# Global queries' scores of a batch in one stage of eight array parts, with masks by two engines, later taps and the second half of the tokens first

## The chip, the cores and the metric

The kernel runs on one core of one Trainium2 chip. The metric is device time in microseconds of one execution; lower is better. Five engines work beside each other and each runs its own instructions in order: TensorE (PE in the profile, PEld for its weight loads), VectorE (DVE), ScalarE (ACT), GpSimd (POOL) and SyncE (SP), which here only issues the DMA transfers.

## What is computed

Attention with 32 global and 512 local tokens per head, then a gated feed-forward block with a convolution of three taps over the tokens. There are 8 batches, 8 heads, 64 numbers per head, 512 model columns and 1024 hidden columns. The reference, cut to what matters:

```python
k_all, v_all = concat([k_g, k_l]), concat([v_g, v_l])        # 32 + 512 tokens
out_g = softmax(scale * q_g @ k_all.T) @ v_all               # global queries see every token
s_ll  = where(abs(i - j) <= 32, scale * q_l @ k_l.T, -1e9)   # local queries: a window
out_l = softmax(concat([scale * q_l @ k_g.T, s_ll])) @ v_all
x = concat([out_g, out_l])                                   # tokens first, heads side by side: 544 rows of 512
h = maximum(x @ w_in, 0.0)
gate = 1 / (1 + exp(-conv3(h, conv_w)))
out = (h * gate) @ w_out
```

## The kernel before, in words

**Attention.** Two heads make a pair, with the first head's 64 numbers in partitions 0 to 63 and the second's in 64 to 127. One transfer (LQ, line 229) brings a pair's queries and its keys, another (LV, line 236) its values, and LG (line 242) four heads' global queries, padded with zeros so that one matmul over 128 partitions picks one head of a pair. The stages of a pair are S (scores, line 264, eight parts of the array of 64 rows x 32 columns), M (scale, mask and minimum on DVE, line 285, four blocks a head), E (exponential on ACT, line 295), T (transposes, line 304), A (copy out of PSUM), P (values, line 325, four parts of 128 x 32), N (division by the sums, line 333), U (transposes, line 341) and, for each half of the 544 tokens, XH and XL (the rounded value and the rest, line 364). Tokens 0 to 271 are the first half; the 32 global tokens are its head.

**Global queries.** For every four heads there is a chain of its own: G (scores against all keys, line 278: four matmuls of 480 columns and four of 64 in four parts of 128 x 32, into two PSUM banks), GM (scale and minimum, lines 373 to 377), GE (exponential), GN (one over the sums, into the small tile `gw`, lines 389 to 392), GT (six transposes, line 406), GC (copies into `pgt`), GP (values, line 422), GO (multiplies by `gw` and places the heads, line 429), GQ (line 436) and GX (lines 443 and 444), which writes the global tokens' columns of the first half. There are 16 such chains, two in a batch.

**Feed-forward.** A unit is 128 hidden columns of one half of a batch's tokens: PZ (twelve matmuls, line 460), RE (line 469), C1 (middle tap on POOL, line 248), Ca and Cb (outer taps on DVE, line 484), and for two units at a time TH (line 493), GG (line 498), GH and GL (the rounded product and the rest). Eight units make a half; then four output tiles follow, each of Oa and Ob (twelve matmuls each, line 523), OE (copy) and ST (store, line 536). The first half's units need GX, the second half's don't.

**Weights.** The weights come as 64-bit numbers in eight pieces of 1024 KB, four of w_in and four of w_out. WD loads a piece (line 174), WA takes its magnitude on ACT (line 112), WC (lines 119 to 123) and WL (lines 126 to 134) turn it on DVE into a rounded part and a rest, WH casts the rounded part on ACT. The taps are treated in the same way ahead of everything else (lines 149 to 159). A piece of w_in serves two units of each half, a piece of w_out one output tile.

**Masks.** POOL builds `corner` and copies it in 30 blocks into `mask` (lines 85 to 105), behind `place` and `whose`.

**Order.** A planner in the kernel (`plan`, `arranged`, `emit`) goes through all stages with a cost table and, for every kind of stage, a due time (`POS` for the batches from the second on, `POS0` for the first, `WPOS` for the weight pieces); the engine takes the most urgent stage that is ready and whose buffers are free (`SLOTS`: 8 PSUM banks, 3 qk, 3 vf, one pg, one pgt and so on). The order that comes out is then fixed on each engine.

Of the kernel before, what the change touches and what calls it, by code (L numbers as in the profile page):

```python
# [47 lines left out]
def f(ap):  # L48
    return ap.bitcast(F32)
# [3 lines left out]
def attn_moe(ctx: ExitStack, tc: tile.TileContext, qk_d, vw_d, qg_d, w_in_d, w_out_d, cw_d, out_d):  # L53
# [19 lines left out]

    place = const.tile([P, 2, SG], F32, name="place")
# [7 lines left out]

    corner = const.tile([P, 2, 4, SG], F32, name="corner")
    nc.gpsimd.memset(corner, 0.0)
    for k, sign in enumerate((1, -1)):
        nc.gpsimd.affine_select(
            out=corner[:, k], in_=corner[:, k], pattern=[[sign * SG, 4], [sign, SG]], compare_op=ALU.is_ge, fill=NEG,
            base=0, channel_multiplier=-sign,  # L90
        )
    mask = const.tile([P, 4, 4, SG], F32, name="mask")
    nc.gpsimd.memset(mask, 0.0)
    for i in range(NB):
        t, b = divmod(i, 4)
        rows = slice(b * SG, (b + 1) * SG)
        for k in range(4):
            block = FIRST[i] + k
            local = block - block // 4
            if block % 4 == 3 or local == i:  # L100
                continue
            if abs(local - i) > 1:
                nc.gpsimd.memset(mask[rows, t, k], NEG)
            else:
                nc.gpsimd.tensor_copy(out=mask[rows, t, k], in_=corner[rows, int(local > i), b])
# [22 lines left out]
    def rest(on, out, w0, w1, p, low):  # L128

        nc.vector.tensor_scalar(out=w1, in0=w1, scalar1=low, scalar2=None, op0=ALU.bitwise_and)  # L130
        v = nc.vector
        v.scalar_tensor_tensor(out=f(w1), in0=w0, scalar=2.0**-32, in1=w1, op0=ALU.mult, op1=ALU.add)  # L132
        if on == "v":
            v.scalar_tensor_tensor(out=out, in0=f(w1), scalar=2.0**-20, in1=f(p), op0=ALU.mult, op1=ALU.mult)
        else:
            nc.scalar.mul(out=f(p), in_=f(p), mul=2.0**-20)
            nc.gpsimd.tensor_tensor(out=out, in0=f(w1), in1=f(p), op=ALU.mult)
# [11 lines left out]
    nc.sync.dma_start(out=cwr.rearrange("p n w -> p (n w)"), in_=cw_d)  # L149
    cw = drop(cwr)  # L150
    if wpe == 2:
        cw = const.tile([P, 3 * NFT], F32, name="cw")
        cwp = const.tile([P, 3 * NFT], U32, name="cwp")
        w0, w1, t = cwr[:, :, 0], cwr[:, :, 1], cw.bitcast(U32)
        magnitude(w1, t)
        scaled_bits(w1, t, 0x7FFFF8)
        power(cwp, t)
        rest("v", f(cwp), w0, w1, cwp, 0)
        nc.vector.tensor_tensor(out=cw, in0=cw, in1=f(cwp), op=ALU.add)
# [24 lines left out]
    def WA(i):  # L184
        if wpe == 2:
            wf[i] = load.tile([P, 1024], U32, name="wt", bufs=SLOTS["wt"])
            magnitude(raw[i][:, :, 1], wf[i])

    def WC(i):
        if wpe == 2:  # L190
            scaled_bits(raw[i][:, :, 1], wf[i], 0x7FF000)
# [4 lines left out]
    def WL(i):  # L196
# [22 lines left out]
    groups = {}  # L219
    xs = {}  # L220
# [17 lines left out]
    def LG(n):  # L238
        b, h = divmod(n, H)
        gr = groups[n // 4] = {}  # L240
        gr["qgf"] = load.tile([P, 4, SG], F32, name="qgf", bufs=SLOTS["qg"])
        nc.sync.dma_start(out=gr["qgf"], in_=qg_d[b, h // 4])
# [26 lines left out]
    def G(n):  # L269

        gr = groups[n // 4]
        gr["s0"] = bank([P, 480], "psg0")
        gr["s1"] = bank([P, 64], "psg1")
        for i, ps in enumerate((gr["s0"], gr["s1"])):
            for j in range(4):
                k = heads[n - 3 + j // 2 * 2]["qk"][:, SL:]
                k = k[:, 608:672] if i else k[:, 0:640].rearrange("p (a c) -> p a c", c=P)[:, :, 0:96]
                nc.tensor.matmul(ps[j * SG : (j + 1) * SG], lhsT=gr["qgf"][:, j, :], rhs=k, start=True, stop=True)  # L278
# [107 lines left out]
    def GN(n):  # L386
# [4 lines left out]
        gr["w"] = small.tile([P, 2], F32, name="gw", bufs=SLOTS["pg"])  # L391
        nc.vector.tensor_scalar(out=gr["w"], in0=whose, scalar1=sums, scalar2=None, op0=ALU.mult)
# [22 lines left out]
    def GP(n):  # L415
        gr, first = groups[n // 4], n - 3
        po = gr["po"] = bank([P, D], "go")
        for c in range(6):
            for j in range(4):
                own = slice(j * SG, (j + 1) * SG)  # L420
                v = heads[first + j // 2 * 2]["vf"][:, j % 2, VALUES.index(ONCE[c]), :]
                nc.tensor.matmul(po[own], lhsT=gr["pgt"][:, c, own], rhs=v, start=c == 0, stop=c == 5)  # L422

    def GO(n):

        gr = groups[n // 4]
        og = gr["og"] = att.tile([P, 2, D], F32, name="og", bufs=SLOTS["pg"])
        po, w = gr["po"], gr["w"]
        nc.vector.tensor_tensor(
            out=og, in0=po[:, None, :].to_broadcast([P, 2, D]), in1=w[:, :, None].to_broadcast([P, 2, D]), op=ALU.mult  # L430
# [19 lines left out]

    def Z(u):
        hh, ft = divmod(u, NFT)
        b, half = divmod(hh, 2)
# [41 lines left out]
    def GG(u):  # L495
        t, half = hid[u]["two"], u // NFT % 2
# [30 lines left out]
    def OE(o):  # L527
        hh, mt = divmod(o, NCT)
        b, half = divmod(hh, 2)
# [3 lines left out]
    def ST(o):  # L533
        hh, mt = divmod(o, NCT)
        b, half = divmod(hh, 2)
# [7 lines left out]
        Oa=lambda o: O(o, 0), Ob=lambda o: O(o, 1), OE=OE, ST=ST, WD=WD, WA=WA, WC=WC, WH=WH, WL=WL,  # L543
# [5 lines left out]
    ps=8, x=13, hb=2, qk=3, vf=3, qg=2, p=4, r=3, a=4, n=2, pg=1, pgt=1, t=2, o=2, wt=1, g0=2, g1=2,  # L549
# [5 lines left out]
    A="a", GC="a", XH="a", GX="v", RE="a", C1="p", GH="a", GL="v", OE="v", WA="a", WH="a", WL="v",  # L555
)
ENG0 = dict(
    A="a", GC="a", XH="a", GX="v", RE="a", C1="p", GH="a", GL="p", OE="v", WA="a", WH="a", WL="v",
# [15 lines left out]
LATE = (17.01, 35.33)
# [346 lines left out]
```

## Time and profile before

| | |
|---|---|
| median of 3 runs | 595.16 us (594.88 to 595.27) |
| the profiled execution's own time | 595.32 us |
| its span, first to last instruction | 593.5 us |
| mean granted TensorE clock | 0.982 |
| PE busy | 560.9 us, 95% |
| DVE, ACT, POOL busy | 424.0, 324.2, 101.1 us |
| moved by DMA | 68.46 MB |

A row of a group names line, engine, operation, tiles written and read, sizes and count, then the busy time in us, the mean of one in ns, and the engine's idle time just ahead of it with what ended it. A row of the timeline gives start and length in us; several alike are merged, and a bracket at the end is idle time before it and its releaser. Matmuls are counted twice where they are of plain fp32: 128 matmuls of G are 256 records. Instructions of one engine overlap a little, so the distance from one start to the next is the measure of what one costs.

### The profile page before, as it was taken

What the parts mean: (1) busy time and instruction counts of PE and PEld (TensorE: products, weight loads), DVE (VectorE), ACT (ScalarE), POOL (GpSimd) and SP (SyncE); (2) the same over time, 40 slices, a digit from 0 to 9 for tenths busy, and PEclk for the clock granted to TensorE, in tenths of its full rate; (3) what the DMA queues carried; (4) which work ended last, traced back from release to release, by engine and by line L of the source; (5) the groups of instructions that cost most, each with busy time, mean ns of one, the idle gap of its engine ahead of it and who ended that gap; (6) DMA issues with size and microseconds to landing.
All of it is one profiled execution on the core that took longest, in us unless ns stands there. A gap on an engine that the chain in (4) does not pass through costs nothing.

```text
span 593.5 us, 20757 instructions
## 1 busy us (share of the span) xinstructions
PE 560.9 (95%) x8704; PEld 528.8 (89%) x8704; DVE 424.0 (71%) x1388; ACT 324.2 (55%) x994; POOL 101.1 (17%) x190
## 2 busy tenths in 40 slices
PE   5656997999999999999999999999999999999997
PEld 3345896999999999999999999999999999999997
DVE  4999999689477948577685858668584856565651
ACT  4954794676477666446565655555565543333320
POOL 6000242033012111121111012111101212221210
PEclk9977999899999999999999999999999999999999
DMA  6987334156234332123333222232412000000001
GB/s 254 390 286 313 95 118 170 39 204 223 91 135 153 107 134 98 56 110 108 135 108 145 100 78 94 100 144 97 146 63 75 20 22 20 29 20 29 30 29 47
DMA packets 22125, 68.46 MB, mean 115 GB/s; under 512 B 2576, under 2 KB 12816, under 8 KB 21008
## 3 DMA queue, kind: packets, MB, share of 16 engines
q1 hardware_dynamic: 22032, 67.14, 31.2%
q8 instruction: 68, 1.11, 0.8%
q14 instruction: 25, 0.20, 0.1%
HBM read 58.22 MB, written 8.91 MB: 113 GB/s over the span
## 4 chain that ended last, share of the span: by engine, by line
PE 84%; DVE 9%; ACT 2%; issue 1%; DMA 1%; POOL 0%; DVEq 0%
PE ps_o L523 32%; PE ps_h L460 31%; PE ps_v L325 5%; PE ps_s L264 4%; PE ps_t L304 4%; PE pv L341 2%; PE psg L278 2%; PE go L422 2%; PE gt L406 1%; DVE pr L285 1%; DVE t L484 1%; DMA vf<-vw 1%; DVE wt L123 1%; DVE raw L132 1%; ACT pr L295 1%
## 5 line engine op out<-in xcount | busy, mean ns | idle before, releaser
L460 PE MATMUL ps_h<-xh,w_in 128*128 128x274 f32 x1024 | 225.4, 298 | 2.8 <-DVE raw L132 1.3
L523 PE MATMUL ps_o<-g,w_out 128*128 128x272 f32 x1536 | 212.2, 290 | 0.0
L523 PEld LDWEIGHTS ps_o<-g,w_out 128*128 128x128 f32 x1536 | 200.0, 189 | 0.2
L460 PEld LDWEIGHTS ps_h<-xh,w_in 128*128 128x128 f32 x1024 | 171.9, 191 | 6.3 <-ACT g L212 1.4
L248 POOL TENSOR_SCALAR t<-hb,cw 128x272 f32<-128x272 f32 x128 | 79.9, 629 | 425.7 <-ACT hb L469 159.2
L460 PE MATMUL ps_h<-xl,w_in 128*128 128x274 f32 x512 | 149.5, 292 | 0.8 <-issue 0.8
L484 DVE SCALAR_TENSOR_TENSOR t<-hb,cw,t 128x272 f32<-128x272 f32 x256 | 125.7, 514 | 30.5 <-POOL t L248 29.1
L295 ACT ACTIVATE pr<-pr,negm 128x128 f32<-128x128 f32 x256 | 99.5, 391 | 47.7 <-DVE negm L285 47.7
L469 ACT ACTIVATE hb<-ps_h 128x273 f32<-128x273 f32 x128 | 50.8, 398 | 93.4 <-PE ps_h L460 91.9
L460 PEld LDWEIGHTS ps_h<-xl,w_in 128*128 128x128 f32 x512 | 98.1, 192 | 1.0 <-issue 1.0
L285 DVE CUSTOM_DVE_ANT_0 pr<-ps_s,mask 128x128 f32<-128x128 f32 x256 | 57.8, 285 | 25.6 <-PE ps_s L264 23.2
L212 DVE COPY o<-ps_o 128x272 f32<-128x272 f32 x64 | 28.0, 438 | 54.8 <-PE ps_o L523 54.6
L212 ACT CAST g<-t 128x544 fp32r<-128x544 f32 x64 | 40.9, 646 | 34.5 <-DVE t L498 22.6
L498 DVE SCALAR_TENSOR_TENSOR t<-t,hb 128x544 f32<-128x544 f32 x64 | 46.0, 719 | 14.3 <-ACT t L493 13.3
L493 ACT ACTIVATE t<-t 128x544 f32<-128x544 f32 x64 | 42.4, 663 | 15.0 <-DVE t L484 13.9
L212 ACT COPY a<-ps_t 128x512 f32<-128x512 f32 x64 | 37.0, 583 | 23.2 <-PE ps_t L304 23.0
L295 ACT ACTIVATION_READ_ACCUMULATOR pr<-pr,negm 128x1 f32 x256 | 48.3, 189 | 0.0
L264 PE MATMUL ps_s<-qk 64*32 64x128 f32 x2048 | 38.4, 283 | 8.4 <-DMA qk<-qk 5.8
L304 PE MATMUL ps_t<-ident,pr 128*128 128x128 f32 x256 | 43.0, 282 | 3.5 <-ACT pr L295 2.5
L215 DVE TENSOR_TENSOR g<-t,g 128x544 fp32r<-128x544 f32 x56 | 41.0, 737 | 6.8 <-ACT g L212 5.3
L264 PEld LDWEIGHTS ps_s<-qk 64*32 64x32 f32 x2048 | 29.9, 109 | 12.7 <-DMA qk<-qk 5.8
L304 PEld LDWEIGHTS ps_t<-ident,pr 128*128 128x128 f32 x256 | 31.1, 144 | 8.2 <-ACT pr L295 7.6
(70 smaller groups left out, 466.1 us busy)
## 6 DMA issues: line engine op xcount, KB each, us to landing
vf<-vw SPq DMA_DIRECT2D x32, 896.0 KB, 6.3
qk<-qk SPq DMA_DIRECT2D x32, 592.0 KB, 4.9
out<-o SPq DMA_DIRECT2D x64, 136.0 KB, 1.7
raw<-w_in SPq DMA_DIRECT2D x4, 1024.0 KB, 6.6
raw<-w_out SPq DMA_DIRECT2D x4, 1024.0 KB, 6.6
qgf<-qg SPq DMA_DIRECT2D x16, 64.0 KB, 2.0
cwr<-cw SPq DMA_DIRECT2D x1, 24.0 KB, 1.9
```

The source lines that it names most:

```text
L212: nc.scalar.copy(out=out, in_=in_) if choice(key) == "a" else eng(key).tensor_copy(out=out, in_=in_)
L248: nc.gpsimd.tensor_scalar(out=out, in0=in_, scalar1=by, scalar2=0.0, op0=ALU.mult, op1=ALU.add)
L264: nc.tensor.matmul(heads[n + j]["s"][b * SG : (b + 1) * SG, t, :], lhsT=qk[rows, i * SG : (i + 1) * SG], rhs=qk[rows, a : a + P], start=Tr ...
L285: nc.vector.tensor_tensor_reduce(out=pr[:, t, :], in0=st["s"][:, t, :], in1=mask[:, t].rearrange("p a c -> p (a c)"), op0=ALU.add, op1=ALU ...
L295: nc.scalar.activation(out=st["p"][:, t, :], in_=st["p"][:, t, :], func=AF.Exp, scale=-1.0, bias=st["m"][:, t : t + 1], accum_out=two["r"] ...
L304: nc.tensor.transpose(out=st["t"][:, t, :], in_=st["p"][:, t, :], identity=ident)
L460: nc.tensor.matmul(ps, lhsT=w[:, ft, ct, :], rhs=x, start=i == 0, stop=i == 3 * NCT - 1)
L469: nc.scalar.activation(out=o, in_=z, func=AF.Relu, scale=0.5)
L484: nc.vector.scalar_tensor_tensor(out=st["t"], in0=st["h"][:, k : k + HALF], scalar=cw[:, 3 * ft + k : 3 * ft + k + 1], in1=st["t"], op0=AL ...
L493: nc.scalar.activation(out=t, in_=t, func=AF.Tanh)
L498: nc.vector.scalar_tensor_tensor(out=t, in0=t, scalar=1.0, in1=h, op0=ALU.add, op1=ALU.mult)
L523: nc.tensor.matmul(ps, lhsT=w[:, mt, ft, :], rhs=g[:, ft, :], start=ft + i == 0, stop=ft == NFT - 1 and i == 2)
```

## The change

- **Global scores.** G runs once per batch. The global queries are no longer padded: LG brings a whole batch, a pair's two heads in the two halves of the partitions. A matmul now has 64 rows; sixteen of them (eight of 480 columns, eight of 64) are issued into eight parts of 64 x 32, and into four PSUM banks at once. The two chains of a batch now hold the even and the odd heads, so GP of four heads takes from both chains' `pgt` and waits for both GC. There are two pg, two pgt and two og buffers, five qk instead of three, and 12 x instead of 13.
- **Scaling.** GN multiplies the whole of `pg` by one over the sums (128 x 544) and no longer makes `gw`; GT now comes behind GN; GO takes the constant `whose` in its place.
- **Masks.** `corner` and `mask` come ahead of `place` and `whose`. DVE clears the mask and writes the blocks of the first two of four row tiles, POOL the others.
- **Taps.** Their load stands behind the load of weight piece 0, and their eight DVE instructions behind that piece's WA.
- **Halves.** With `TURN = 1` the units and outputs of a batch run for the second half of the tokens first.
- **Weights.** A second way to split a piece (`WAY`, stages WS and WT) is added in the code; all eight pieces keep the old way ("vvvvvvvv"), so it is not used.
- **Due times** are all new, a PE stage in the same array form is preferred by 2.0 instead of 1.0, and the planner's costs of G and GN are adapted.

```diff
 def LG(n):
-    gr["qgf"] = load.tile([P, 4, SG], F32, name="qgf", bufs=SLOTS["qg"])
-    nc.sync.dma_start(out=gr["qgf"], in_=qg_d[b, h // 4])
+    qg[n // H] = load.tile([P, 4, SG], F32, name="qgf", bufs=SLOTS["qg"])
+    nc.sync.dma_start(out=qg[n // H], in_=qg_d[n // H])
...
 def G(n):
-    gr["s0"] = bank([P, 480], "psg0")
-    gr["s1"] = bank([P, 64], "psg1")
-    for i, ps in enumerate((gr["s0"], gr["s1"])):
-        for j in range(4):
-            k = heads[n - 3 + j // 2 * 2]["qk"][:, SL:]
-            k = k[:, 608:672] if i else k[:, 0:640].rearrange("p (a c) -> p a c", c=P)[:, :, 0:96]
-            nc.tensor.matmul(ps[j * SG : (j + 1) * SG], lhsT=gr["qgf"][:, j, :], rhs=k, start=True, stop=True)
+    first = n - 7
+    g = [groups.setdefault(2 * (n // H) + j, {}) for j in range(2)]
+    for i, (name, w) in enumerate((("s0", 480), ("s1", 64))):
+        for j in range(2):
+            g[j][name] = bank([P, w], f"psg{i}")
+        for c in range(4):
+            k = heads[first + 2 * c]["qk"][:, SL:]
+            for j in range(2):
+                rows = slice(j * D, (j + 1) * D)
+                kj = k[rows, 608:672] if i else k[rows, 0:640].rearrange("p (a c) -> p a c", c=P)[:, :, 0:96]
+                nc.tensor.matmul(
+                    g[j][name][c * SG : (c + 1) * SG], lhsT=qg[n // H][rows, c, :], rhs=kj, start=True, stop=True
+                )
...
 def GN(n):
-    gr["w"] = small.tile([P, 2], F32, name="gw", bufs=SLOTS["pg"])
-    nc.vector.tensor_scalar(out=gr["w"], in0=whose, scalar1=sums, scalar2=None, op0=ALU.mult)
+    nc.vector.tensor_scalar(out=gr["pg"], in0=gr["pg"], scalar1=sums, scalar2=None, op0=ALU.mult)
...
+    e = nc.vector if t < 2 else nc.gpsimd
...
-        nc.gpsimd.tensor_copy(out=mask[rows, t, k], in_=corner[rows, int(local > i), b])
+        e.tensor_copy(out=mask[rows, t, k], in_=corner[rows, int(local > i), b])
...
 def WD(i):
+    if i == 0:
+        nc.sync.dma_start(out=cwr.rearrange("p n w -> p (n w)"), in_=cw_d)
...
 def WA(i):
+    if i == 0:
+        taps()
...
+def half_of(hh):
+    return (hh + TURN) % 2
...
-    at_n("GT", [("GE", n)], [("ps", f"gt{g}"), ("ps", f"gu{g}")], [f"pg{g}"])
+    at_n("GT", [("GN", i)], [("ps", f"gt{k}"), ("ps", f"gu{k}")], [f"pg{k}"], i=i)
...
-    ps=8, x=13, hb=2, qk=3, vf=3, qg=2, p=4, r=3, a=4, n=2, pg=1, pgt=1, t=2, o=2, wt=1, g0=2, g1=2,
+    ps=8, x=12, hb=2, qk=5, vf=3, qg=2, p=4, r=3, a=4, n=2, pg=2, pgt=2, og=2, t=2, o=2, wt=1, g0=2, g1=2,
...
-WPOS = [11.57, -8.05, 1.24, 15.47, 1.38, 33.08, 13.87, 67.5]
+WPOS = [5.39, -21.72, 2.32, 16.52, -8.61, 49.14, 9.48, 81.09]
```

What the new due times make of the order is shown at three places. First SP, at the start of the program, before (`cwr` is the taps, `qgf` the global queries, `qk` a pair's queries and keys, `raw` a weight piece, `vf` a pair's values):

```order
L149 DMA cwr<-cw 128x48
L242 DMA qgf<-qg 128x128 x2
L229 DMA qk<-qk 128x1184 x2
L174 DMA raw<-w_in 128x2048
L229 DMA qk<-qk 128x1184
L242 DMA qgf<-qg 128x128
L229 DMA qk<-qk 128x1184
L174 DMA raw<-w_in 128x2048
L236 DMA vf<-vw 128x1792
```

And SP at the start of the changed program:

```order
L263 DMA qgf<-qg 128x128
L174 DMA raw<-w_in 128x2048
L252 DMA qk<-qk 128x1184 x2
L263 DMA qgf<-qg 128x128
L252 DMA qk<-qk 128x1184 x2
L174 DMA raw<-w_out 128x2048
L259 DMA vf<-vw 128x1792 x3
```

A weight piece now stands ahead of the first qk, four qk come ahead of the second piece, and the taps' load has gone to the seventeenth place of the queue, behind piece 0. Second, DVE at the start of the program, before (the rows of line 285 are the first masking):

```order
L209 MEMSET hb_156 128x2 x2
L119 TENSOR_SCALAR cw<-cw 128x24
L120 TENSOR_SCALAR cw<-cw 128x24
L123 SCALAR_TENSOR_TENSOR cw<-cwr,cw 128x24
L126 TENSOR_SCALAR cwp<-cw 128x24
L130 TENSOR_SCALAR cwr<-cwr 128x24
L132 SCALAR_TENSOR_TENSOR cwr<-cwr 128x24
L134 SCALAR_TENSOR_TENSOR cwp<-cwr,cwp 128x24
L159 TENSOR_TENSOR cw<-cw,cwp 128x24
L285 ISA pr,negm<-ps_s,mask 128x128
```

And DVE at the start of the changed program (lines 120 to 124 are WC of the first weight piece, line 312 the first masking):

```order
L82 MEMSET mask 128x512
L231 MEMSET hb_145 128x2 x2
L231 MEMSET hb_146 128x2 x2
L93 MEMSET mask 32x32
L95 COPY mask<-corner 32x32 x15
L120 TENSOR_SCALAR wt<-wt 128x1024
L121 TENSOR_SCALAR wt<-wt 128x1024
L124 SCALAR_TENSOR_TENSOR wt<-raw,wt 128x1024
L312 ISA pr,negm<-ps_s,mask 128x128
```

The taps have left this place (they now stand behind the third weight piece), DVE's half of the masks has come in, and one WC has moved ahead of the first masking. Third, PE around G in the fifth or a later batch, before (`ps_v` is stage P, `psg` G, `ps_h` a hidden unit; `gt` follows behind three more units, three output stages, two T and one U):

```order
L325 MATMUL ps_v<-vf,a 32x64 x32
L278 MATMUL psg_4698<-qk,qgf 32x480 x4
L278 MATMUL psg_4699<-qk,qgf 32x64 x4
L460 MATMUL ps_h<-xh,w_in_151 128x274
L460 MATMUL ps_h<-xl,w_in_151 128x274
```

And PE at the same kind of place of the changed program:

```order
L352 MATMUL ps_v<-vf,a 32x64 x32
L303 MATMUL psg_4414<-qk,qgf 32x480
L303 MATMUL psg_4415<-qk,qgf 32x480
...
L303 MATMUL psg_4424<-qk,qgf 32x64
L303 MATMUL psg_4425<-qk,qgf 32x64
```

The matmuls of G now take turns between two banks, sixteen in all, and between them and the first `gt` stand one output stage, one unit, one T and one unit.

More of the change, by code (lines that the diff above doesn't have):

```diff
@@ L70, in attn_moe @@
     make_identity(nc, ident)
+    corner = const.tile([P, 2, 4, SG], F32, name="corner")
+    nc.gpsimd.memset(corner, 0.0)
+    for k, sign in enumerate((1, -1)):
+        nc.gpsimd.affine_select(
+            out=corner[:, k], in_=corner[:, k], pattern=[[sign * SG, 4], [sign, SG]], compare_op=ALU.is_ge, fill=NEG,
+            base=0, channel_multiplier=-sign,
+        )
+    mask = const.tile([P, 4, 4, SG], F32, name="mask")
+    nc.vector.memset(mask, 0.0)
+    for i in range(NB):
+        t, b = divmod(i, 4)
+        e = nc.vector if t < 2 else nc.gpsimd
+        rows = slice(b * SG, (b + 1) * SG)
+        for k in range(4):
+            block = FIRST[i] + k
+            local = block - block // 4
+            if block % 4 == 3 or local == i:
+                continue
+            if abs(local - i) > 1:
+                e.memset(mask[rows, t, k], NEG)
+            else:
+                e.tensor_copy(out=mask[rows, t, k], in_=corner[rows, int(local > i), b])
     place = const.tile([P, 2, SG], F32, name="place")
@@ L153, in attn_moe, with taps @@
         cwp = const.tile([P, 3 * NFT], U32, name="cwp")
[L154 to L159, printed above, removed]
+    def taps():
+        if wpe == 2:
+            w0, w1, t = cwr[:, :, 0], cwr[:, :, 1], cw.bitcast(U32)
+            magnitude(w1, t)
+            scaled_bits(w1, t, 0x7FFFF8)
+            power(cwp, t)
+            rest(f(cwp), w0, w1, cwp, 0)
+            nc.vector.tensor_tensor(out=cw, in0=cw, in1=f(cwp), op=ALU.add)
     def eng(key):
@@ L417, in GP @@
         po = gr["po"] = bank([P, D], "go")
-        for c in range(6):
+        b, h = divmod(first, H)
+        for k in range(6):
             for j in range(4):
-                own = slice(j * SG, (j + 1) * SG)
-                v = heads[first + j // 2 * 2]["vf"][:, j % 2, VALUES.index(ONCE[c]), :]
-                nc.tensor.matmul(po[own], lhsT=gr["pgt"][:, c, own], rhs=v, start=c == 0, stop=c == 5)
+                c = h // 2 + j // 2
+                v = heads[first + j // 2 * 2]["vf"][:, j % 2, VALUES.index(ONCE[k]), :]
+                nc.tensor.matmul(
+                    po[j * SG : (j + 1) * SG], lhsT=groups[2 * b + j % 2]["pgt"][:, k, c * SG : (c + 1) * SG], rhs=v,
+                    start=k == 0, stop=k == 5,
+                )
     def GO(n):
         gr = groups[n // 4]
-        og = gr["og"] = att.tile([P, 2, D], F32, name="og", bufs=SLOTS["pg"])
-        po, w = gr["po"], gr["w"]
+        og = gr["og"] = att.tile([P, 2, D], F32, name="og", bufs=SLOTS["og"])
         nc.vector.tensor_tensor(
-            out=og, in0=po[:, None, :].to_broadcast([P, 2, D]), in1=w[:, :, None].to_broadcast([P, 2, D]), op=ALU.mult
+            out=og, in0=gr["po"][:, None, :].to_broadcast([P, 2, D]), in1=whose[:, :, None].to_broadcast([P, 2, D]),
+            op=ALU.mult,
         )
@@ L495, in GG @@
     def GG(u):
-        t, half = hid[u]["two"], u // NFT % 2
+        t, half = hid[u]["two"], half_of(u // NFT)
         h = hb[u // 2 % SLOTS["hb"]][:, :, half + 1 : half + 1 + HALF]
@@ L658, in op @@
         if names:
-            e = dict(p=PE, s=SP, a=ACT)[names[0]]
-            c = "v"
+            e = dict(p=PE, v=DVE, g=POOL, s=SP, a=ACT)[names[0]]
+            c = WAY[i] if key == "WL" else "v"
         else:
@@ L725, in plan, with weight @@
     return ops
+def weight(i):
+    return ("WL" if WAY[i] == "v" else "WT", i)
 def units(op, late, b):
```

152 lines of the change are left out of this document (76 added, 76 removed).

## The prediction

> **What bounds the kernel now.** I read the page's head first, then the busy time by stretches of 20 us, then the timeline of the stretches where something is lost. One execution of 595.32 us was profiled, 0.16 us above the median of the runs shown; its span is 593.5 us, so 1.8 us lie outside the span, and I carry them over unchanged.
>
> ```profile
> PE 560.9 (95%) x8704; PEld 528.8 (89%) x8704; DVE 424.0 (71%) x1388; ACT 324.2 (55%) x994; POOL 101.1 (17%) x190
> ```
> ```profile
> 0.00:20.00 20.00, 11.37 (x294) 7.72 (x298) 11.09 (x71) 11.01 (x35) 9.48 (x54) 1.00 0.78 298
> 20.00:40.00 20.00, 13.81 (x350) 9.87 (x342) 19.29 (x52) 17.11 (x57) 0.00 (x0) 0.91 0.89 338
> 40.00:60.00 20.00, 11.78 (x221) 8.96 (x222) 19.48 (x44) 8.38 (x20) 1.05 (x1) 0.68 0.76 286
> ...
> 100.00:120.00 20.00, 17.40 (x277) 15.99 (x269) 13.22 (x57) 12.21 (x42) 0.49 (x1) 0.91 0.33 109
> 120.00:140.00 20.00, 20.00 (x475) 18.31 (x465) 18.21 (x67) 15.52 (x54) 6.61 (x8) 1.00 0.46 178
> ...
> 560.00:580.00 20.00, 20.00 (x161) 20.00 (x160) 10.72 (x20) 5.57 (x11) 2.35 (x4) 1.00 0.12 42
> ```
>
> The columns after the length are PE, PEld, DVE, ACT, POOL, the granted clock, the DMA share and GB/s. Two regimes stand out. From 120 us to the end PE is busy 20.00 of 20 us at full clock while DVE has time over: there only less work on PE shortens anything. From 20 to 60 us DVE is full (19.29 and 19.48 of 20) and PE has gaps: there the end is set by how early DVE delivers the weight pieces and the first attention outputs. So I price the change twice: by DVE's list up to a point that both kernels share, and by the PE work that is left behind that point.
>
> **The shared point.** In both orders PE can start the seventh hidden unit (two units per piece of w_in) only when DVE has finished the fourth piece of w_in, and in both PE has done exactly six units and no output stage by then. Before, that is at 74.7 us: the profile has PE waiting there (first row; the second is DVE's next instruction behind the piece).
>
> ```profile
> 73.80 0.36 PE L460 MATMUL ps_h<-xh,w_in 128*128 128x274 f32 x1 [1.27 <-DVE raw L132]
> ```
> ```profile
> 74.73 0.72 DVE L498 SCALAR_TENSOR_TENSOR t<-t,hb 128x544 f32<-128x544 f32 x1
> ```
>
> **Start.** The first scores wait for qk, the first maskings for the masks:
>
> ```profile
> 5.81 3.67 PE L264 MATMUL ps_s<-qk 64*32 64x128 f32 x128 [5.81 <-DMA qk<-qk]
> 7.97 0.29 DVE L285 CUSTOM_DVE_ANT_0 pr<-ps_s,mask 128x128 f32<-128x128 f32 x1 [3.37 <-PE ps_s L264]
> ...
> 11.25 0.29 DVE L285 CUSTOM_DVE_ANT_0 pr<-ps_s,mask 128x128 f32<-128x128 f32 x1 [1.31 <-POOL mask L105]
> ...
> 14.00 0.65 DVE L373 TENSOR_SCALAR_CACHE_REDUCE pg<-psg 128x480 f32<-128x480 f32 x1
> ```
> ```profile
> 5.00:10.00 5.00, 4.19 (x136) 3.51 (x140) 0.81 (x6) 0.90 (x5) 4.45 (x26) 1.00 1.00 396
> ```
> ```profile
> L112 ACT ACTIVATE wt<-raw 128x1024 f32<-128x1024 f32 x8 | 9.3, 1162 | 8.8 <-DVE w_in L134 5.6 <-DVE w_out L134 3.2
> L105 POOL COPY mask<-corner 32x32 f32<-32x32 f32 x30 | 5.4, 203 | 0.7
> ```
>
> Before, DVE ran three maskings while POOL was still writing masks and went on without a stop from 11.25 us. Afterwards POOL copies 15 blocks instead of 30, 15 x 0.2 = 3 us less, and DVE copies the others in time in which it waits anyway; the masks leave the path. What comes in their place is the load: SP now issues a 1024 KB weight piece ahead of the first qk. Before, 24 + 128 + 592 = 744 KB had to move for the first scores at 5.81 us; now 64 + 1024 + 592 = 1680 KB, and 936 KB more at 396 GB/s are 2.4 us: scores at 8.2, first masking (2.16 us behind, as before) at 10.4 us. The weight piece itself lands at about 5.81 + (1088 - 744) / 396 = 6.7 us; ACT's 1.16 us and DVE's first half of its preparation, 2.55 us (next rows), end at 10.4 us too, in a time when DVE has nothing else. So DVE runs without a stop from 10.4 us; between 9.5 (ACT and DVE a little earlier) and 12 us (loads slower).
>
> **DVE's list from there to the fourth w_in piece.** These rows price it; the distance from one start to the next is what an instruction takes of DVE:
>
> ```profile
> 15.23 0.64 DVE L119 TENSOR_SCALAR wt<-wt 128x1024 f32<-128x1024 f32 x1
> ...
> 17.78 0.28 DVE L285 CUSTOM_DVE_ANT_0 pr<-ps_s,mask 128x128 f32<-128x128 f32 x1
> ...
> 33.41 0.68 DVE L333 TENSOR_TENSOR n<-ps_v,sums 128x512 f32<-128x512 f32 x1
> 34.01 0.40 DVE L364 TENSOR_TENSOR xl<-pv,xh 128x242 fp32r<-128x242 f32 x1
> 34.33 0.16 DVE L315 TENSOR_SCALAR sums<-sums 128x8 f32<-128x8 f32 x1
> ...
> 34.65 0.64 DVE L119 TENSOR_SCALAR wt<-wt 128x1024 f32<-128x1024 f32 x1
> ...
> 37.19 0.65 DVE L373 TENSOR_SCALAR_CACHE_REDUCE pg<-psg 128x480 f32<-128x480 f32 x1
> ...
> 38.11 0.41 DVE L364 TENSOR_TENSOR xl<-pv,xh 128x242 fp32r<-128x242 f32 x1
> ```
> ```profile
> 2.88 0.33 DVE L119 TENSOR_SCALAR cw<-cw 128x24 f32<-128x24 f32 x1 [1.92 <-ACT cw L112]
> ...
> 4.42 0.18 DVE L159 TENSOR_TENSOR cw<-cw,cwp 128x24 f32<-128x24 f32 x1
> ```
>
> Before, DVE goes from 11.25 to 74.73 us, 63.5 us. Counted in the two orders, the new list differs so: 52 maskings instead of 41 (44 less the three already run), at (14.00 - 11.25) / 13 = 0.21 us each, +2.3; one first half of a weight piece less, 17.78 - 15.23, -2.55; the taps, which stood in idle time and now stand in the list, 4.42 + 0.18 - 2.88, +1.7; one more normalisation +0.60, two more differences 2 x 0.32 = +0.64, one more pair of sums +0.32; one evaluation GM less, 38.11 - 37.19, -0.92; and GN scales 544 columns of pg where it scaled two of gw. That form is not in the trace: it costs at least nothing, and at most what the 1024 wide rows of L119 take (0.7 us); I take +0.2 us each, +0.4 here. Sum: +2.5 us. The fourth piece is ready at 10.4 + 63.5 + 2.5 = 76.4 us, **1.7 us later** than before.
>
> **What PE has left at that point.** One steady stretch gives the pitches, the groups the two stages that it lacks:
>
> ```profile
> 366.07 1.16 PE L264 MATMUL ps_s<-qk 64*32 64x128 f32 x64
> 367.16 1.10 PE L325 MATMUL ps_v<-vf,a 128*32 128x64 f32 x64
> 368.08 1.10 PE L278 MATMUL psg<-qk,qgf 128*32 128x480 f32 x16
> 369.11 0.39 PE L460 MATMUL ps_h<-xh,w_in 128*128 128x274 f32 x1
> ...
> 370.75 0.60 PE L304 MATMUL ps_t<-ident,pr 128*128 128x128 f32 x4
> 371.19 0.60 PE L341 MATMUL pv<-ident,n 128*128 128x128 f32 x4
> 371.54 1.75 PE L523 MATMUL ps_o<-g,w_out 128*128 128x272 f32 x12
> ```
> ```profile
> L422 PE MATMUL go<-vf,pgt 128*32 128x64 f32 x768 | 14.4, 221 | 2.3 <-ACT pgt L212 1.5 <-issue 0.8
> L406 PE MATMUL gt<-ident,pg 128*96 128x128 f32 x96 | 13.8, 282 | 0.8 <-ACT pg L382 0.8
> ```
>
> The new order has done one stage S more (1.09), three transposes T (3 x 0.44), one P (0.92) and one U (0.35), but one GT (13.8 / 16 = 0.86) and one GP (14.4 / 16 = 0.90) fewer: 3.7 - 1.8 = 1.9 us less is left. And the stages G: before, 13 of 16 are left, 13 x 1.03 = 13.4 us; afterwards 7 of 8. A new one has sixteen matmuls of 64 rows in eight parts where an old one has eight of 128 rows in four. If the two row halves run side by side for nothing, a batch costs 1.03 us as one old group does. The stage that already runs eight parts is S: 32 x 128 = 4096 columns in 1.09 us; at that pace G's 8 x 480 + 8 x 64 = 4352 columns take 1.16 us. If the halves run one behind the other it is 2.06. S is the nearest row, and its 1.09 holds a change of array form, so I take 1.10: 7.7 us, and **5.7 us less**. Together PE has 7.6 us less left, at a point 1.7 us later: -5.9 us.
>
> **What else is lost behind the point.** Before, PE lost time once more, at 100 us:
>
> ```profile
> 103.48 0.88 PE L264 MATMUL ps_s<-qk 64*32 64x128 f32 x41 [2.60 <-issue]
> ...
> 106.58 2.54 PE L523 MATMUL ps_o<-g,w_out 128*128 128x272 f32 x12
> 108.95 0.60 PE L341 MATMUL pv<-ident,n 128*128 128x128 f32 x4
> ```
>
> It waited 2.60 us for nothing that the profile shows, and ran slowly behind it: one hidden unit and one output stage took from 104.36 (the end of the first row) to 108.95, 4.6 us, where two units take 2 x 1.64 us (369.11 to 370.75 above), 1.3 us less. No reason ties these 3.9 us to the old order or frees the new one of them; I take half, -2.0 us. Against that stands a shorter distance in the steady state: between G and the first GT PE now has only two hidden units, one output and one T (some 5 us at these pitches), while DVE has to do GM twice (0.92 each), one GG and one GL (0.7 each, by the row at 74.73) and GN (0.6 by the pieces above), 3.8 us with ACT's exponential beside them, and GT now waits for GN. About 1 us is spare; I put +1 us over the seven batches for it. Second half first, four qk and three vf in SP's queue, `whose` in GO, one x slot fewer: I cost them at nothing, since the steady-state transfers are hidden: between the first GP and the P that needs the slot which it frees stand four units, four output stages and two S, 14 us of PE work.
>
> Sum: 595.3 - 5.9 - 2.0 + 1.0 = **588.4 us**, chance 0.62.
>
> **Rivals.** (1) *GT comes too late*, the one that ends slower. In each of seven batches PE would stand still at the first GT. It decides from the point where DVE reaches GM 2.2 us late: 1 us is spare, and (7 + 1.2) / 7 = 1.2 us per batch eat the gain and 0.2% more. At 2.5 us late it costs 7 x 1.5 = 10.5 us more than forecast, about 599 us. For it: DVE works in order, and eight maskings stand just ahead. Against it: DVE is 71% busy and waits for PE's outputs in the steady state. Chance 0.08. (2) *The eight parts don't overlap*: 7 x 2.06 = 14.4 us of G instead of 7.7, 6.7 us more: 595 us, no change. S's pace speaks against it; chance 0.05. (3) *G waits for banks.* Before, a G takes two of eight banks, now four at once, and the chain before GP holds more. The old G has next to no wait ahead of it, so two banks were always free; nothing shows that four are. If each of the seven waits half a unit, 0.75 us, it is 588.4 + 5.2 = 593.6 us; chance 0.10. [...] The trace of S, which splits rows into two banks as well, has only 8.4 us of PE idle time in 32 stages, 5.8 of them the first load, so I leave it small. (4) *The prologue comes out better*: DVE starts at 9.5 us and the whole 4.2 us are gone, 588.4 - 0.9 - 2.0 - 1 = 584.5 us or a little less; chance 0.15.
>
> ```profile
> L278 PE MATMUL psg<-qk,qgf 128*32 128x480 f32 (+1 forms) x256 | 18.6, 411 | 0.0
> L264 PE MATMUL ps_s<-qk 64*32 64x128 f32 x2048 | 38.4, 283 | 8.4 <-DMA qk<-qk 5.8 <-issue 2.6
> ```
>
> **Numbers.** The forecast's own bounds (start 9.5 to 12, G 1.03 to 1.16, the stall wholly back or wholly gone, GT 0 to 3 us) make 583 to 592. With rival 4 below and rival 3 above, 582 to 594 leaves out only the rivals of no change and of slower, 0.13, and the tails. Faster by over 0.2% (below 594.0): 0.62 + 0.10 + 0.15 = 0.87; within 0.2%, about what a measurement of this kernel can tell from no change: 0.05; slower: 0.08.
>
> **What would show it.** Right: `psg` busy about 9 us in all instead of 18.6; the seventh unit starting near 76 us; PE busy 20.00 of 20 us from 120 us on. Wrong: G at 2 us per batch; PE idle ahead of `gt` or `psg` in every batch; DVE waiting for a load or for ACT between 10 and 75 us, most of all ahead of the fourth pair's normalisation, whose vf comes only after the first GP has freed a slot.

## The result and the profile after

The changed kernel takes 605.62 us (median of 4 runs, 602.82 to 608.16), the kernel before 595.02 us (4 runs) beside it: a ratio of 1.0168, 95% interval 1.0143 to 1.0192. It is slower by 1.7%, and outside the range. The profiled execution took 602.82 us, its span is 601.0 us, 7.5 us more than before. First the page's busy row, then the same stretches by 20 us as before the change (PE, PEld, DVE, ACT, POOL, granted clock, DMA share, GB/s):

```profile
PE 557.3 (93%) x8704; PEld 529.7 (88%) x8704; DVE 431.9 (72%) x1405; ACT 325.0 (54%) x994; POOL 95.6 (16%) x175
```
```profile
20.00:40.00 20.00, 12.36 (x266) 9.68 (x258) 19.07 (x63) 16.63 (x55) 0.00 (x0) 0.83 0.75 292
40.00:60.00 20.00, 13.84 (x380) 11.26 (x380) 18.24 (x58) 12.11 (x39) 0.00 (x0) 0.74 0.83 328
...
400.00:420.00 20.00, 18.79 (x360) 18.08 (x359) 12.20 (x45) 11.20 (x38) 1.59 (x3) 1.00 0.32 108
420.00:440.00 20.00, 20.00 (x217) 19.76 (x217) 13.88 (x39) 10.02 (x29) 3.65 (x6) 1.00 0.07 23
```

PE is busy 3.6 us less than before, yet the span is longer: PE stands still more. And it does so where it was full before, in the steady state: 18.79 of 20 us in one stretch, 20.00 in the next. The timeline shows where in the stretch:

```profile
407.01 1.10 PE L352 MATMUL ps_v<-vf,a 128*32 128x64 f32 x64
407.93 0.85 PE L449 MATMUL go<-vf,pgt 128*32 128x64 f32 x48
408.71 1.94 PE L285 MATMUL ps_s<-qk 64*32 64x128 f32 x117
411.86 0.44 PE L285 MATMUL ps_s<-qk 64*32 64x128 f32 x11 [1.21 <-issue]
```

P, GP and two S now stand next to each other: 240 records of short matmuls in a row. After 229 of them PE stops for 1.21 us, in the middle of a stage whose inputs are all there, and the releaser is "issue": nothing that the profile shows. Ten such waits lie behind 100 us, 0.71 to 1.39 us each, 11.2 us together; before there were three, 4.2 us (the 2.60 us at 103.48, 0.78 and 0.79). The waits by releaser (total, times, longest) name the line, and the lines of the two stages that I had doubted show nothing:

```profile
PE ps_s L285 <- issue: 10.2, 9, 1.3
```
```profile
L432 PE MATMUL gt<-ident,pg 128*96 128x128 f32 x96 | 13.4, 279 | 0.0
L303 PE MATMUL psg<-qk,qgf 64*32 64x480 f32 (+1 forms) x256 | 9.8, 417 | 0.0
```
```profile
390.96 1.15 PE L303 MATMUL psg<-qk,qgf 64*32 64x480 f32 x32
392.03 1.78 PE L556 MATMUL ps_o<-g,w_out 128*128 128x272 f32 x12
```

G is what the prediction took it for: 9.8 us in all instead of 18.6, a batch in 392.03 - 390.96 = 1.07 us, never waiting for banks, and GT never waiting for G's chain. The other shortfall is early. The shared point, where the seventh hidden unit gets its weight piece, has gone from 74.87 to 78.79 us (the first row below is from before, the second from the changed kernel); and DVE, which was to run without a stop from 10.4 us, started on time but stopped three times for ACT (further rows, the changed kernel):

```profile
74.87 0.53 PE L460 MATMUL ps_h<-xh,w_in 128*128 128x274 f32 x2 [0.57 <-DVE w_in L134]
78.79 0.82 PE L493 MATMUL ps_h<-xh,w_in 128*128 128x274 f32 x2 [2.99 <-DVE w_in L134]
```
```profile
7.36 0.69 DVE L120 TENSOR_SCALAR wt<-wt 128x1024 f32<-128x1024 f32 x1 [1.16 <-ACT wt L113]
...
19.49 0.17 DVE L342 TENSOR_SCALAR sums<-sums 128x8 f32<-128x8 f32 x1 [1.11 <-ACT pr L322]
...
35.81 0.41 DVE L391 TENSOR_TENSOR xl<-pv,xh 128x242 fp32r<-128x242 f32 x1 [0.42 <-ACT xh L234]
43.83 0.18 DVE L120 TENSOR_SCALAR cw<-cw 128x24 f32<-128x24 f32 x1 [1.21 <-ACT cw L113]
```

So the 7.5 us come out as +3.9 at the shared point and +3.6 behind it. Summed up by stage, from each stage's start to the next one's, PE's work behind the point is 5.7 us less; the seventh unit itself, behind its 2.99 us wait, takes 1.2 us more (its pairs of matmuls last 0.66 us, those of other units 0.42); and idle time is 12.6 us instead of 4.5, +8.1.

### The profile page after: what moved, and what is told of

It reads as the page before. It is cut to its first block, busy times and chain, and to the rows that moved or that the text cites. A ratio compares the mean times of both kernels' runs of the same rounds, so it can differ in the third digit from the quotient of the medians.

```text
span 601.0 us, 20745 instructions
## 1 busy us (share of the span) xinstructions
PE 557.3 (93%) x8704; PEld 529.7 (88%) x8704; DVE 431.9 (72%) x1405; ACT 325.0 (54%) x994; POOL 95.6 (16%) x175
## 3 DMA queue, kind: packets, MB, share of 16 engines
q8 instruction: 68, 1.11, 0.8%
## 4 chain that ended last, share of the span: by engine, by line
PE 83%; DVE 12%; issue 2%; ACT 1%; DMA 1%; SPq 0%
PE ps_o L556 33%; PE ps_h L493 31%; PE ps_s L285 5%; PE ps_v L352 4%; PE ps_t L331 4%; PE pv L368 2%; DVE pr L312 2%; PE gt L432 2%; PE go L449 2%; DVE wt L124 1%; DVE raw L133 1%; PE psg L303 1%; DMA raw<-w_in 1%; DVE w_in L134 1%; DVE t L517 1%
## 5 line engine op out<-in xcount | busy, mean ns | idle before, releaser
L269 POOL TENSOR_SCALAR t<-hb,cw 128x272 f32<-128x272 f32 x128 | 75.8, 594 | 436.2 <-ACT hb L502 334.1
L285 PE MATMUL ps_s<-qk 64*32 64x128 f32 x2048 | 39.9, 288 | 18.1 <-issue 10.2
L285 PEld LDWEIGHTS ps_s<-qk 64*32 64x32 f32 x2048 | 31.7, 111 | 23.0 <-issue 13.5
L331 PE MATMUL ps_t<-ident,pr 128*128 128x128 f32 x256 | 41.1, 283 | 2.1 <-ACT pr L322 1.6
L352 PE MATMUL ps_v<-vf,a 128*32 128x64 f32 x2048 | 38.3, 227 | 4.5 <-ACT a L234 3.1
```

The lines of the kernel that those rows point to most:

```text
L269: nc.gpsimd.tensor_scalar(out=out, in0=in_, scalar1=by, scalar2=0.0, op0=ALU.mult, op1=ALU.add)
L285: nc.tensor.matmul(heads[n + j]["s"][b * SG : (b + 1) * SG, t, :], lhsT=qk[rows, i * SG : (i + 1) * SG], rhs=qk[rows, a : a + P], start=Tr ...
L331: nc.tensor.transpose(out=st["t"][:, t, :], in_=st["p"][:, t, :], identity=ident)
L352: nc.tensor.matmul(ps[rows, t, j, :], lhsT=heads[n + j]["a"][:, t, rows], rhs=heads[n]["vf"][:, j, VALUES.index(FIRST[4 * t + b]), :], sta ...
```

## The experiments

**Theory.** The theory, at this point a guess from the stop after 229 records of a run of 240, is that TensorE's own instructions run out: short matmuls would use them up faster than they come, and in a run of some 200 PE would have to wait for more. The change made the runs longer: the order counts seven of 240 and one of 288, where before there were two of 192 and eleven of 176. The cause in the change would be the preference for stages of the same array form (`STAY` 2.0 instead of 1.0) and the new due times. **Rival:** PSUM banks: three stages of short matmuls in a row and G's four banks leave none free for the second S, and the profile doesn't show that wait.

**e1: break the runs.** Of the changed kernel only the order on PE is touched: in seven places the output stage that follows the run is moved into it, between GP and the first S.

```diff
+        if sum(short[ops[j][0]] for j in run) > 200 and m < len(pe) and ops[pe[m]][0] == "Ob":
+            first = [j for j in run if ops[j][0] == "S"][0]
+            seq.remove(pe[m])
+            seq.insert(seq.index(first), pe[m])
```

> The changed kernel with seven output stages (second halves, Ob) moved one place forward on TensorE, between GP and the two S behind it, so that the seven runs P+GP+S+S of 240 matmul records become 112 and 128; nothing else differs. Theory 'supply' (TensorE's own instructions run dry in long runs of short matmuls): the seven waits of 0.7 to 1.3 us inside these runs go, idle time put down to 'issue' behind 100 us falls from 11.2 us to under 4, time 605.6 - 8 = about 597 us. Rival 'banks' (the second S waits for PSUM banks or for another release that the profile does not show): S waits as before, 602 us or more.

Measured: 596.33 us (10 runs; before 594.61 beside it), ratio 1.0041, interval 1.0011 to 1.0071, where the changed kernel has 1.0168. The same place in its timeline:

```profile
402.85 1.10 PE L352 MATMUL ps_v<-vf,a 128*32 128x64 f32 x64
403.77 0.85 PE L449 MATMUL go<-vf,pgt 128*32 128x64 f32 x48
404.55 1.77 PE L556 MATMUL ps_o<-g,w_out 128*128 128x272 f32 x12
406.26 2.06 PE L285 MATMUL ps_s<-qk 64*32 64x128 f32 x128
```

No wait is left here. Both S follow each other as before and take the same banks. That alone does not refute the banks, since both S now come 1.7 us later; the place of the waits does. By the kernel's code a stage S writes both its banks from its first two matmuls on, so a wait for a bank would stand ahead of these; the six waits in runs of 240 stand behind 40 to 60 of the 64 records of a stage S. Behind 100 us three waits remain, 3.2 us instead of 11.2. Most of the loss is explained and undone, 1.3 of 1.7%; but not even then is the kernel faster than before.

**e2 and e3: the preference alone.** `STAY` back at 1.0 (longest runs in the steady state: five of 176) and at 0.5 (none over 128 there); the due times stay new.

```diff
-STAY = 2.0
+STAY = 1.0
```

> The changed kernel with the preference for stages of the same array form set back from 2.0 to 1.0; the order comes out anew from about the fourth batch: five runs of 176 records in place of seven of 240, the first batches' runs of 192 to 288 unchanged. Supply: at most one or two waits of 0.8 us behind the third batch, some 0.2 us per added change of form on the other side, about 598 us. Banks: as many waits ahead of S as in the changed kernel, 602 us or more.

> The changed kernel with the preference at 0.5: no run above 128 records behind the prologue, more changes of array form than with 1.0. Supply: no wait put down to 'issue' behind 120 us but for the 192 runs of the second batch; about 597 us, within 2 us of the kernel with 1.0. Banks: waits ahead of S remain, 602 us or more.

Measured: 600.79 us, ratio 1.0085 (1.0053 to 1.0118), with waits for "issue" of 5.1 us behind 100 us; and 597.51 us, ratio 1.0041 (1.0014 to 1.0069), with one of 1.8 us. Time follows the length of the runs, by a second way of shortening them. The preference that the change doubled is thus a cause, not the due times alone. The length of one run is not the whole measure, though: in a single stage S of 64 records PE stops after 51 in the changed kernel (0.75 us, at 124.18 us), in e2 (2.28 us) and in e3 (1.80 us). Ahead of that S stand a run of 112, one hidden unit, a P and a U.

**e4: TensorE by itself.** A kernel that computes nothing of the reference: PE runs 112 to 640 short matmuls in a row, in the form of stage P, with 60 long ones (274 columns) between the runs; first with nothing else on the chip's queues, then beside 60 loads of 896 KB.

> Only TensorE at work: runs of 112, 144, 176, 208, 240, 288, 384 and 640 records of matmuls like P's (128x32, 64 columns), each behind at least 60 full matmuls of 274 columns, once without and once with 896 KB loads under way; no engine waits for another, the output is not the reference's. Supply: no idle time in the runs of 112 and 144; from some length between 150 and 240 a wait of about 1 us, later in the same run another, and a lower pace in the run of 640 than in the run of 112; longer with the loads under way. Banks: no idle time at any length and one pace for all.

Six rows of the first half, and four of the second (start, length, records, idle time before):

```profile
54.33 2.66 PE L83 MATMUL ps_short<-v,a 128*32 128x64 f32 x176
...
64.91 2.32 PE L83 MATMUL ps_short<-v,a 128*32 128x64 f32 x151
68.42 1.00 PE L83 MATMUL ps_short<-v,a 128*32 128x64 f32 x57 [1.19 <-issue]
...
121.77 1.99 PE L83 MATMUL ps_short<-v,a 128*32 128x64 f32 x128 [1.01 <-issue]
125.50 1.99 PE L83 MATMUL ps_short<-v,a 128*32 128x64 f32 x128 [1.74 <-issue]
128.95 1.99 PE L83 MATMUL ps_short<-v,a 128*32 128x64 f32 x128 [1.46 <-issue]
...
176.76 1.76 PE L83 MATMUL ps_short<-v,a 128*32 128x64 f32 x111
179.41 1.11 PE L83 MATMUL ps_short<-v,a 128*32 128x64 f32 x65 [0.89 <-issue]
...
237.41 3.64 PE L83 MATMUL ps_short<-v,a 128*32 128x64 f32 x239
245.26 3.64 PE L83 MATMUL ps_short<-v,a 128*32 128x64 f32 x128 [4.21 <-issue]
```

Without loads 112, 144 and 176 pass without a wait, 208 stops after 151 records, 288 after 223 (240 happened to pass), and the run of 640 stops after 199 and from there on after every 128. Beside loads 176 already stops, after 111, and the waits grow to 4.2 us (in the last pair the granted clock is lower too, 0.50 from 245 to 249 us). The buffers are of no account here: two banks, which nobody reads until the end. So the wait comes from PE's instructions alone, in portions of 128 records, and data loads make it longer.

The portions can be seen. The page counts the transfers by queue (packets, MB, share of 16 engines), and one of them is for instructions; below it the same view of the changed kernel for 409 to 410 us, just ahead of the wait that ends at 411.86:

```profile
q8 instruction: 68, 1.11, 0.8%
```
```profile
q1 hardware_dynamic: 8, 0.06, 33.8%
q8 instruction: 1, 0.02, 8.0%
```

PE has 8704 matmuls and as many weight loads, 17,408; over the 68 packets of q8 that is 256 each on average, or 128 matmuls with their weight loads, the portion after which the run of 640 stops. Narrowing the window places the packets: in the run of 640 of e4 without loads at 119.33, 122.77, 126.58 and 130.31 us, 3.4 to 3.8 us apart, and beside loads, around the run of 384, at 236.61, 242.70, 249.03 and 255.27, 6.1 to 6.3 us apart. It is the loads and not the clock that stretch this distance: once they have ended, at 269.6 us, the packets come at 270.18, 274.08, 277.52 and 281.32, 3.4 to 3.9 us apart again, though the granted clock is still 0.50 from 269 to 273 us. PE uses a portion of short matmuls up in 1.99 us (3.64 us where the clock is 0.50). And the packets fit the waits: each of the 69 waits for "issue" of more than 0.15 us in the twelve profiles of this case ends 2.1 to 2.9 us after a packet of this queue starts, the wait at 411.86 us 2.8 us after one at 409.04. So short matmuls use a portion up faster than the next one comes: 1.99 us of use against 3.4 to 3.8 us between packets without loads, and 3.64 (at a granted clock of 0.50) against 6.1 to 6.3 beside loads.

**e5: the changed code with the old due times** and the old preference of 1.0.

```diff
-STAY = 2.0
+STAY = 1.0
...
 POS = dict(
-    LQ=-3.62, LG=-73.86, LV=-8.61, S=-5.17, M=14.83, E=81.37, NS=-90.03, T=-2.74, A=-62.12, P=-21.52, N=-10.33,
...
+    LQ=-3.56, LG=-53.13, LV=12.71, S=-3.9, M=7.61, E=46.84, NS=-11.03, T=-16.54, A=-39.33, P=-1.74, N=0.2, U=-7.02,
...
```

> The changed code (global scores of a batch in one stage, masks, taps, second half first, buffers) with the due times and the preference of 1.0 of the kernel before. Its longest unbroken run of short matmuls behind the first 100 us is 128, against 240 in the changed kernel. If the loss comes from the new due times through the long runs (my theory), the waits of 0.7 to 1.4 us behind 100 us are nearly gone (at most 3 us in all, against 11.2) and the time is 588 to 593 us, below the kernel before. If the changed code itself costs (stages G, the scaling in GN, the halves turned round), it is at 597 us or above with no such waits.

Measured: 604.42 us, ratio 1.0162 (1.0136 to 1.0188): neither case. Waits for "issue" behind 100 us are 3.5 us, close to the 3 us that the theory allowed, but the time is the rival's. The three waits stand in runs of 112 and 64 records (the longest, 1.73 us at 234.13, behind 92 of 112), so here too the length of one run is not the whole measure. The time is lost early, on DVE: in this order more attention stands ahead of the units, and PE waits for DVE as late as 91 us.

```profile
91.65 0.34 PE L303 MATMUL psg<-qk,qgf 64*32 64x64 f32 x14 [3.57 <-DVE xl L391]
```
```profile
80.00:100.00 20.00, 15.78 (x172) 13.10 (x169) 19.69 (x60) 16.20 (x52) 5.66 (x6) 0.83 0.33 117
```

Before, PE was busy 19.62 us in that stretch and had done more than ten units and four output stages by 100 us; here it had done nine units and not one whole output stage. In the steady state the code does no harm. The distance between G stages gives what one batch takes (means over three or four batches): before 68.4 us, changed kernel 69.7, e1 67.7, e2 68.2, e3 68.1, e5 67.9. That is 0.2 to 0.7 us a batch in favour of the new code (e2 and e3 the least), where long runs don't eat it. So the run doesn't tell the due times' fault from the code's in the whole, only in the steady state; code and first-batch due times seem to fit each other, so that they can't be exchanged singly.

**e6: the kernel before, its two longest runs broken.** The next hidden unit is moved into both runs of 192.

```diff
+        if sum(short[ops[j][0]] for j in run) > 180:
+            seq.remove(pe[m])
+            seq.insert(seq.index(run[2 if ops[run[-1]][0] == "G" else 1]), pe[m])
```

> The kernel before, with one hidden unit moved into each of its two runs of 192 short matmuls, so that they become 64 and 128. If TensorE's instructions run dry in long runs, the wait of 2.60 us at 103 us goes and with it the slow clock behind it: 3 to 4 us less, about 591.5 us. If that wait has another cause (a load, the place in the program), it stays and the time is 595 us, or up to 0.5 us more for the added change of array form.

Measured: 593.14 us, ratio 0.9973 (0.9953 to 0.9992): faster than before, by half of what was expected. At the place of the 2.60 us a wait of half the size is left:

```profile
104.61 1.07 PE L264 MATMUL ps_s<-qk 64*32 64x128 f32 x53 [1.30 <-issue]
```

The direction is the theory's. That one unit ahead of P and S is too short a pause for the instructions to catch up would explain the rest; no run here varies the pause alone, so that is argued, not shown.

**e7: e1 with the taps at the start,** as before the change.

```diff
     cw = drop(cwr)
+    nc.sync.dma_start(out=cwr.rearrange("p n w -> p (n w)"), in_=cw_d)
...
+    taps()
...
-        if i == 0:
-            taps()
```

> The kernel with the broken runs (596.3 us), with the taps loaded and prepared at the start, as before the change. If DVE's list sets the shared point (the seventh hidden unit, at 79.0 us there), it loses the taps' 1.7 us and the 1.21 us wait for ACT, gains about 0.6 us ahead of the first weight piece, and the point comes at 76.7 us, the time at 594.0 us. If the point is set by the loads (SP's queue), it stays at 79 and the time at 596.

Measured: 595.01 us, ratio 1.0012 (0.9991 to 1.0033). PE's shared point, and what DVE now waits for:

```profile
77.55 0.83 PE L492 MATMUL ps_h<-xh,w_in 128*128 128x274 f32 x2 [3.00 <-DVE w_in L134]
```
```profile
20.27 0.17 DVE L341 TENSOR_SCALAR sums<-sums 128x8 f32<-128x8 f32 x1 [1.49 <-ACT pr L321]
```

The point comes 1.5 us earlier instead of 2.3: DVE's list does set it, the wait for the taps is gone, and the wait for the exponentials at 20 us has grown from 1.11 to 1.49, because ACT, not DVE, is late there.

**e8: e7 with two more runs broken,** both of 192, by the unit that follows.

```diff
+        elif sum(short[ops[j][0]] for j in run) == 192 and ops[pe[m]][0] == "PZ":
+            seq.remove(pe[m])
+            seq.insert(seq.index(run[2]), pe[m])
```

> The changed kernel with the broken runs and the taps at the start (595.0 us), with two more runs of 192 short matmuls (S, S, P and P, S, S around 120 and 160 us) broken by the hidden unit that follows them. If the instructions run dry in long runs, the waits of 1.44 us at 124.7 and 1.22 us at 161.5 us go, for two added changes of array form of about 0.17 us: about 592.7 us. If the waits only move to the next long stage, 594.5 to 595 us.

Measured: 593.37 us (12 runs; before 595.70 beside it), ratio 0.9964 (0.9947 to 0.9981). With the long runs and the taps put right, the changed kernel beats the kernel before. Waits for "issue" behind 100 us are down to 1.85 us; one of the two has moved into the unit, as the second case said:

```profile
159.07 0.29 PE L492 MATMUL ps_h<-xl,w_in 128*128 128x274 f32 x1 [1.29 <-issue]
```

**e9: e6 with the masks by two engines,** and with `corner` and `mask` ahead of `place` and `whose`: a part of the change that leaves the planner's order alone.

```diff
-    nc.gpsimd.memset(mask, 0.0)
+    nc.vector.memset(mask, 0.0)
...
+        e = nc.vector if t < 2 else nc.gpsimd
...
-                nc.gpsimd.tensor_copy(out=mask[rows, t, k], in_=corner[rows, int(local > i), b])
+                e.tensor_copy(out=mask[rows, t, k], in_=corner[rows, int(local > i), b])
```

> The kernel before with its two runs of 192 broken (593.1 us), and of the change only the masks by two engines, with corner and mask ahead of place and whose. If the masks bound DVE's start, DVE goes on without a stop from about 8.0 us instead of 10.6 (11.25 us less the three maskings it had done), the seventh hidden unit starts 2 to 2.6 us earlier (before: 74.9 us), and the time is about 590.8 us. If the loads or PE are late next, the point moves by less than 1 us and the time stays at 592.5 to 593.5.

Measured: 590.93 us (6 runs; before 595.70), ratio 0.9930 (0.9906 to 0.9954), the best of all kernels here. DVE's first masking, behind which it doesn't stop for masks any more, and the shared point:

```profile
8.33 0.29 DVE L285 CUSTOM_DVE_ANT_0 pr<-ps_s,mask 128x128 f32<-128x128 f32 x1 [0.75 <-PE ps_s L264]
```
```profile
72.57 0.52 PE L460 MATMUL ps_h<-xh,w_in 128*128 128x274 f32 x2 [0.37 <-DVE w_in L134]
```

The point comes at 72.57 us, 2.3 earlier than before (2.0 earlier than in e6), and the time is 2.6 us less than e6's (0.9973 - 0.9930, of 595). The masks bound the start, and DVE's list carries the gain to PE undiminished. It does so although PE stood still for "issue" 5.9 us in all ahead of the point (3.79 us of it at 38.01 us), where e6 has no such wait: up to the point it is DVE that sets the time.

**e10: the kernel before, eleven runs broken,** to price the cure: the rule of e6 from 150 records on (the edit is shown against e6).

```diff
-        if sum(short[ops[j][0]] for j in run) > 180:
+        if sum(short[ops[j][0]] for j in run) > 150 and n > 60:
```

> The kernel before with eleven runs of 176 and 192 broken by a hidden unit (the two of 192 and nine of 176), so that all runs behind 60 us are at most 144. It prices the added changes of array form. The waits of 0.84 and 0.56 us that are left with two runs broken (593.1 us) should go, 1.4 us. If a change of array form costs what the units ahead of P show against those ahead of another unit (1.70 to 1.72 against 1.55, 0.16 us), nine of them take 1.4 us back: 593.1 us again. If they cost nothing, 591.7 us; if breaking doesn't stop the waits, 594.5 us.

Measured: 597.29 us, ratio 1.0026 (1.0010 to 1.0042), slower than before, where each of the cases expected it faster. The waits of 0.84 and 0.56 us are gone, but in each of eight places behind 200 us a new one stands:

```profile
353.13 0.39 PE L460 MATMUL ps_h<-xh,w_in 128*128 128x274 f32 x1
...
354.85 1.10 PE L325 MATMUL ps_v<-vf,a 128*32 128x64 f32 x64
355.76 0.85 PE L422 MATMUL go<-vf,pgt 128*32 128x64 f32 x48
357.05 0.43 PE L436 MATMUL gq<-place,og 128*128 128x64 f32 x2 [0.44 <-DVE og L429]
```

The unit that was moved away had covered GO on DVE between GP and GQ: 0.44 us. The change of array form costs beside it: the unit ahead of P takes 354.85 - 353.13 = 1.72 us against 1.64 before, and GP and GQ some 0.07 and 0.1 us more, about 0.26 us. Eight times 0.7 us is 5.6 us for 1.4 us of waits saved, 4.2 us net, where the ratios of e10 and e6 differ by 3.2 us (1.0026 - 0.9973, of 595). Breaking paid where PE had stopped for 2.60 us (e6), and not where the stage moved away had covered a wait of 0.44 us (e10).

## Why the prediction was wrong, point by point

- **"What else is lost behind the point" is the step that failed.** I wrote of the 2.60 us wait for nothing that the profile shows that "no reason ties these 3.9 us to the old order or frees the new one of them", and booked half of it as a gain, -2.0 us. A reason ties it: the long run in which it stands. It was the one place of the old order where S, P and S made 192, with loads beside it; a packet of the instruction queue starts at 101.2 us, 2.3 us before the wait ends, and with the run broken half of the wait went (e6). The new order has seven of 240, and idle time behind the point went up by 8.1 us: 10.1 of the 14.4 us by which the span was missed. I had the row, its 41 records behind a stop in mid-stage, and the doubled preference for the same array form in the diff, and costed the latter at nothing.
- **The start** (10.4 us, bounds 9.5 to 12): right. WC begins at 7.36 us and with its three rows ends at about 10.
- **The shared point** (1.7 us later): 3.9 us later. The list's length was right, "without a stop" was not: 1.11, 0.42 and 1.21 us of waits for ACT, 2.7 us. The taps, taken at 1.7 us, cost another 1.21 us because ACT takes their magnitude when its own queue gets to it. e7 gave 1.5 us back. I counted DVE's work and not what ACT has to deliver to it.
- **PE's work** (7.6 us less): 5.7 us less behind the point without the seventh unit, and 1.2 us more in that unit. G's term was right, 5.9 us against 5.7, and psg at 9.8 us met the sign. Summed by stage, T came out better (3.1 us less, not 1.3), P worse (0.6 us more, not 0.9 less) and S worse (0.2 us less, not 1.1). What I left out is the stage next door: a unit ahead of P takes 1.70 us, ahead of an output stage 1.57, and behind 130 us about 100 units and outputs stand ahead of an attention stage instead of some 75. Units alone are 1.6 us more.
- **GT** (+1.0 us): it never waited (0.0 in its row). The spare time was enough.
- **Rivals.** (1) GT too late, (2) parts that don't overlap and (3) banks are all refuted by G's and GT's rows (0.0 us of idle time ahead of both, G busy 9.8 us in all). (4) A better prologue didn't come in the changed kernel, but e9 shows that the masks had it to give. The slower outcome came from none of the four.
- **Signs.** "PE busy 20.00 of 20 us from 120 us on" was the one that told: 18.66 to 19.29 in the stretches in which a run of 240 stops.
- **The range.** The forecast's own bounds, all at their low or all at their high ends, add up to 584.1 and 594.4 us, not to the 583 and 592 that I wrote. The profiled execution's 602.82 us lies above both.

Open is why the changed kernel's own runs spread by 5 us (602.82 to 608.16). Waits that depend on when loads and instruction packets meet would do that: the order of e10 is that of e6 up to 156 us, and yet the profile of e10 has waits of 1.08, 2.42 and 1.99 us up to there and that of e6 one of 1.30. No run here separates loads from packets.

## What to carry to other kernels

A wait in the middle of a stage with no releaser is a question to answer before it is booked as a gain: count the instructions ahead of it, and look for the instruction queue among the transfers. An order that groups small matmuls to save changes of array form had a ceiling here: without loads PE first stopped behind 151 to 259 records in a row, beside data loads behind 111 to 239 (e4), and sooner where a single unit of long ones separates two groups (behind 51 of an S at 124.18 us of the changed kernel); beyond it the grouping cost more than it saved (605.62 us, and 596.33 with the seven runs broken). And a list that bounds an engine must be priced with what other engines have to hand to it, item by item.

## What the runs showed of the hardware

- The instruction queue q8 has 68 packets for 17,408 matmuls and weight loads, 256 each on average, or 128 matmuls and their weight loads; in e4's run of 640 PE stops after 199 records and from there on after every 128. In runs long enough to stop PE a packet comes every 3.4 to 3.8 us with idle DMA, and every 6.1 to 6.3 us beside loads; 128 short matmuls take 1.99 us, 3.64 at a granted clock of 0.50 (e4). Each of the 69 waits for "issue" in the profiles ends 2.1 to 2.9 us after such a packet starts.
- 60 long matmuls of 274 columns take 8.0 us in e4; at that pace 128 take 17 us (an estimate), against 3.4 to 6.3 us from packet to packet. A stage of long ones behind a long run was still the one that waited at two places (0.90 us at 110.46 us in e4, three long matmuls behind the run of 384; 1.29 us at 159.07 us in e8).
- In the changed kernel's seventh unit, behind 2.99 us of waiting, pairs of matmuls take 0.66 us instead of 0.42, at a granted clock of 0.50 from 78.8 to 81.0 us.
- Sixteen matmuls in eight parts of 64 x 32 take 1.07 us (changed kernel, from 390.96 to 392.03 us) where eight in four parts of 128 x 32 take 1.03 (before, from 368.08 to 369.11): the row halves do run side by side here.
